# A hash-attention and gated feed-forward kernel: x of the last but one pair in a ring place, and other steps where the two stages meet

## The chip, the cores and the metric

The kernel runs on one core of a Trainium2 chip. The metric is the device time of one execution in microseconds (us); the lower, the better.

## The reference

Two blocks follow each other, all in fp32:

```python
q_bits = (einsum('bhsd,dk->bhsk', q, proj) > 0)       # 6 bits; the same for k
mask = q_bucket[:, :, :, None] == k_bucket[:, :, None, :]
scores = where(mask, q @ k.T / sqrt(64), -1e9)
attn = softmax(scores)                                # + 1e-9 in the denominator
x = (attn @ v).transpose(0, 2, 1, 3).reshape(3072, 512)
out = (silu(x @ w_gate) * (x @ w_val)) @ w_out
```

q, k and v are 4 batches x 8 heads x 768 x 64; w_gate and w_val are 512 x 1536, w_out is 1536 x 512.

## The kernel before, in words

The order of instructions on every engine is the order in which the program writes them (a manual schedule); semaphores do the rest.

**Attention.** The work goes by pairs of heads: 4 batches x 4 pairs, n = 0 to 15. For each pair, TensorE (PE) forms scores in 12 units (2 halves of 384 queries x 6 chunks of 128 keys, `score`, line 550), ACT takes the exponential (line 560), DVE adds the weights up (`add`, lines 599 to 606), and PE multiplies them with v (`attend`, line 581). Pair 0 is special: q and k land in two halves each, are copied into `qraw` and `kraw` (`start_first`, line 470), are transposed on PE (line 485), and are copied to `qT` and `kT` (lines 489 and 492).

The softmax denominators take a way of their own. `total(n)` sums them on PE (line 617), `fetch_row` copies the row on ACT (622) and sends it by DMA to `few`; `invert` takes the reciprocal on DVE (630), sends it to DRAM (`sums`) and loads it back spread over the partitions, by two DMAs, into the tile `r` (639). `norm` then scales x of that pair on DVE (646), and for pairs of batch 1 to 3 stores it in DRAM (`xram`, line 650). The list `waiting` holds inversions still to come, `last` scalings still to come; `settle` turns the first into the second, `finish` runs a list.

**Preparing the weights.** The weights come as doubles, in 36 pieces of 128 x 512. Each is loaded into a `words` tile, scaled on ACT (lines 139, 140), widened on DVE (lines 153, 155, 158: "widening", `widen_pieces`), rounded on ACT (146), split on DVE into parts (166, 168), and stored in DRAM as `ram`. In the attention this is done in batches (`begin_pieces`, `widen_pieces`, `keep_pieces`); in the gated block `turns()` gives it out in single steps, seven for each piece. In all, 22 pieces are kept when the gated block begins.

**Gated block.** Tokens go in blocks of 1024 (3 blocks). An order written out by hand alternates up steps U (12 per block, each with a gate half and a value half of 24 matmuls: 16 into `a`, 8 into `n`) and down products D (after U3, U6, U9 and U11; 8 chunks of 9 matmuls each into one tile `o` of two PSUM banks; the last one of a block starts four chunks ahead). All products come from one pool `pp` of four such tiles. After the first half of an up step, ACT copies `a` (779), DVE subtracts `n` (785); after the second, DVE multiplies the two (789), ACT writes `hid` (790), and two more DVE steps on `hid` (796, 799) are put off until after the next atom. Each chunk of a first down product is copied by ACT (840) and finished by DVE (846).

Each of these pieces of work, two per half of an up step and one per chunk, is an "atom" and counts one in `count[0]`. After each atom a number of preparing steps is given out, from the tuple by `kind`. The list `left` holds what remained of the attention's inversions and scalings; it is taken up at atoms 6 and 14.

**Ring.** Weights for PE are loaded from `ram` by POOL's queue into a ring of six places (`bring`, line 251), three in a pool of the whole kernel and three in `late_ring`, a pool in memory that the attention held. `hid`, `gate` and `val` lie in the attention's memory too. Three pieces are brought in the last three rounds of the attention, three at the start of the gated block, and one after each half of an up step, three after each down product. POOL's queue also carries the weight loads and stores of the attention; SP's queue carries q, k, v, the small DMAs of the denominators, and later the weights (`queues[0]`).

Of the kernel before, what the change touches and what calls it, by code (L numbers as in the profile page):

```python
# [8 lines left out]
FP32 = mybir.dt.float32  # L9
# [10 lines left out]
def kernel(  # L20
# [20 lines left out]
    nc = tc.nc  # L41
# [62 lines left out]
    n = 0  # L104
# [136 lines left out]
    def bring(count=1):  # L241
        for _ in range(count):
            i = len(held)
            if i == len(wanted):
                return
            what, n = wanted[i]
            at = place[what, n % NF]
            assert progress["kept"] > at, (i, at, progress)
            pool = ringp[i % sum(RINGS) >= RINGS[0]]
            held[what, n] = t = pool.tile([P, 3, PIECE], FP32R, tag="ring", name="ring")  # L250
            nc.gpsimd.dma_start(t.bitcast(FP32), ram[at].bitcast(FP32))  # L251

# [52 lines left out]
    def attention(scope):  # L305
# [127 lines left out]
        def front(n):  # L433
            bits["q", n] = sides["q", n % 2]
            bits["k", n] = sides["k", n % 2]
            low, high = slice(0, BLOCK), slice(D, D + BLOCK)

            def hash_blocks(todo):
                tile_ = joint(n - 2)[:, 1]
                for i, (name, half) in enumerate(todo):  # L440
                    nc.tensor.matmul(tile_[i * BLOCK : (i + 1) * BLOCK, 0:HQ], hash_w,  # L441
                                     T[name, n][:, half * HQ : (half + 1) * HQ],
                                     start=True, stop=True)

                def sign(i, name, half, to=low, **how):
                    nc.scalar.activation(bits[name, n][to, half * HQ : (half + 1) * HQ],
                                         tile_[i * BLOCK : (i + 1) * BLOCK, 0:HQ], AF.Sign,
                                         **(how or {"bias": nudge[name]}))

                return [lambda i=i, at=at, **how: sign(i, *at, **how) for i, at in enumerate(todo)]  # L450

            def spread_k(times, cols=slice(0, S)):
                b = bits["k", n][:, cols]
                for to, by in ((high, times[1]), (low, times[0])):
                    nc.vector.tensor_scalar(b[to], b[low], scalar1=by, scalar2=None, op0=ALU.mult)

            def spread_q():
                nc.scalar.dma_start(bits["q", n][high], bits["q", n][low])

            def hash_next(todo):  # L460
                q0, q1, k0, k1 = hash_blocks(todo)
                return [q0, q1, spread_q, k0, k1, lambda: spread_k(times_k)]

            def transpose_blocks(name):
                T[name, n] = opnd.tile([P, S], FP32, tag=name + "T", name=name + "T")
                nc.vector.transpose(T[name, n], raws[name, n].rearrange("p c h d -> p (c h d)"))

            def start_first():
                def copy(how, name, at):
                    how(raws[name, n].rearrange("p c h d -> p h c d")[:, :, at],  # L470
                        landing[name][:, :, at])

                copy(nc.scalar.copy, "k", slice(0, 1))
                copy(nc.vector.tensor_copy, "k", slice(1, CH))
                copy(nc.vector.tensor_copy, "q", slice(0, CH))
                copy(nc.vector.tensor_copy, "k", slice(CH, NCH))
                copy(nc.vector.tensor_copy, "q", slice(CH, NCH))
                for half in range(2):
                    cols = slice(half * HQ, (half + 1) * HQ)
                    for name in "kq":  # L480
                        if not half:
                            T[name, n] = opnd.tile([P, S], FP32, tag=name + "T", name=name + "T")
                        ps = two_banks("tps")[:, 0]
                        for i in range(CH):
                            nc.tensor.transpose(ps[:, i * P : (i + 1) * P],
                                                raws[name, n][:, half * CH + i].rearrange("p h d -> p (h d)"),
                                                ident)
                        if name == "k":
                            nc.scalar.activation(T[name, n][:, cols], ps[:, 0:HQ], AF.Copy,
                                                 scale=2 / OFF)  # L490
                        else:
                            nc.vector.tensor_copy(T[name, n][:, cols], ps[:, 0:HQ])

                tile_ = joint(n - 2)[:, 1, 0:HQ]
                products(0)
                hash_blocks([("k", 0), ("q", 0), ("k", 1), ("q", 1)])
                signs = twos[-1][:, 1, 1, 0 : HQ // 2].bitcast(BF16)
                nc.scalar.activation(signs, tile_, AF.Sign, bias=every[:, 0:1])

                def spread(half, at):  # L500
                    rows = slice(2 * half * BLOCK, (2 * half + 1) * BLOCK)
                    to = slice(half * HQ + at.start, half * HQ + at.stop)
                    for i, here in enumerate((low, high)):
                        nc.vector.tensor_scalar(bits["k", n][here, to], signs[rows, at],
                                                scalar1=every[rows, 1 + i : 2 + i], scalar2=None,
                                                op0=ALU.mult)

                def copy_q(half, copy, here):
                    rows = slice((2 * half + 1) * BLOCK, (2 * half + 2) * BLOCK)
                    copy(bits["q", n][here, half * HQ : (half + 1) * HQ], signs[rows])  # L510

                copy_q(0, nc.scalar.copy, low)
                spread(0, slice(0, P))
                copy_q(0, nc.vector.tensor_copy, high)
                spread(0, slice(P, HQ))
                spread(1, slice(0, HQ))
                for here in (low, high):
                    copy_q(1, nc.vector.tensor_copy, here)
                products(1)
                products(2)  # L520
                mark(0)
                products(3)
                for i in range(1, 4):
                    mark(i)

            order = [("q", 0), ("q", 1), ("k", 0), ("k", 1)]
            if n:
                return [lambda name=name: transpose_blocks(name) for name in "kq"] + [
                    lambda: hash_next(order)]
            return start_first()  # L530
# [3 lines left out]
        av = {}  # L534
        xT = {}
        mean = {}
        waiting = []

        def weights(u):
# [33 lines left out]
        def attend(u):  # L573
# [7 lines left out]
                nc.tensor.matmul(ps[h * D : (h + 1) * D, 0:width], raws["v", n][:, h, c, :],  # L581
                                 a[:, h, 0:width], start=c == 0, stop=c == NCH - 1)
            if (half, c) == (1, NCH - 1):
                pool, tag = (xp, "xT") if n < len(pairs) - 1 else (lastp, "last")
                xT[n] = pool.tile([P, S], FP32, tag=tag, name=tag)
                mean[n] = small.tile([P, 1], FP32, tag="e", name="e")
                nc.scalar.activation(mean[n], av[n][:, 0, HQ : HQ + 1], AF.Copy, scale=EPS)
                nc.scalar.copy(xT[n].rearrange("p (x q) -> p x q", x=2), av[n][:, :, 0:HQ])
# [40 lines left out]
        def invert(n, few):  # L629
# [2 lines left out]
            nc.sync.dma_start(s, few)  # L632
            if n == len(pairs) - 1:
                t = homes[-1].tile([P, 2, DM], FP32, tag=f"o{NP - 1}", name="o")[:, :, 0:HQ]
            else:
                t = att.tile([P, 2, HQ], FP32, tag="r", name="r", bufs=1)
            flat = s.rearrange("p e -> (p e)").rearrange("(h x t) -> h (x t)", h=2, t=HQ)
# [37 lines left out]
        for n in range(len(pairs)):  # L675
# [4 lines left out]
            if n and more:  # L680
                steps = front(n + 1)
                prepare_pair(2)
            widen_pieces()
            settle()
            for i in range(2 * NCH):
                if u + i > 3:
                    score(u + i)
# [21 lines left out]
                attend(u + c)  # L709
            load(n + 2, "v")  # L710
            keep_pieces()
            if n >= len(pairs) - 3:
                bring()
        widen_pieces()
        settle()
        total(len(pairs) - 1)()
        finish(last)
        left.extend(waiting)

    left = []  # L720
    homes = []
# [6 lines left out]
    def gated_block(scope):  # L728
# [39 lines left out]
        def atoms_of(kind, n):  # L768
            if kind == "U":
# [5 lines left out]
                for what, z in (("g", gate), ("v", val)):  # L775
# [5 lines left out]
                    def other(what=what, z=z):  # L781
                        _, second, _, n_ = ops[what]
                        second()
                        bring()
                        nc.vector.tensor_tensor(two(z), two(z), n_, op=ALU.subtract)  # L785
                        if what == "g":
                            nc.scalar.activation(z, z, AF.Silu)  # L787
# [104 lines left out]
                    yield chunk  # L892

        bring(RINGS[1])
        queues[0] = nc.sync
        tails = []
        splits = []
# [20 lines left out]
        for kind, n in order:  # L918
# [12 lines left out]
            for at, atom in enumerate(atoms_of(kind, n)):  # L931
# [12 lines left out]
                        for x in more:  # L944
                            x.pop(0)()
                count[0] += 1
                if left and count[0] in (6, 14):
                    left.append(left.pop(0)())
                    left[:] = [f for f in left if f]
                for _ in range(((1, 2, 2, 2) if kind == "U" else (1, 2, 2) + (1,) * 9)[at]):  # L950
                    step = next(mine, None)
                    if step:
                        step()
# [35 lines left out]
```

## Time and profile before

| | us |
|---|---|
| time before, median of 3 (909.69 to 911.08) | 910.63 |
| the profiled execution: its own time | 911.15 |
| the profiled execution: its span | 909.3 |
| PE busy in the span | 902.5 |
| DVE busy | 665.9 |
| ACT busy | 449.7 |
| POOL busy | 90.3 |
| gated block's first matmul | 314.22 |
| PE's last matmul ends | 903.70 |

The span goes from the first to the last instruction; the time has 1.85 us more around it. PE's busy time is made of modelled ends, so the distance between starts says more than the busy share. In lines of the timeline the first number is the start, the second the duration, both in us; the bracket gives the idle time of that engine just before and what ended it.

### The profile page before, as it was taken

To read this page: it belongs to the slowest core of one execution; us is meant where nothing else is said; L and a number is where in the kernel's file an instruction comes from. 1 tells how busy PE (TensorE), PEld (TensorE's weight loads), DVE (VectorE), ACT (ScalarE), POOL (GpSimd) and SP (SyncE) were. 2 spreads that over 40 slices of the span, in tenths; PEclk is the share of its full clock that TensorE was granted. 3 is DMA by queue.
4 is the path that set the end of the run, shared out by engine and by line. 5 is a ranking of instruction groups with operands and counts; after the bars stand their busy time and mean duration, and the time that the engine had idled before them with its cause. 6 is when DMAs were issued, how large, how long until landed. Compare 5 with 4: busy or idle time off the path is not lost.

```text
span 909.3 us, 12462 instructions
## 1 busy us (share of the span) xinstructions
PE 902.5 (99%) x4801; PEld 638.0 (70%) x4801; DVE 665.9 (73%) x785; ACT 449.7 (49%) x603; POOL 90.3 (10%) x186
## 2 busy tenths in 40 slices
PE   9999999999999999999999999999999999999998
PEld 5444444444444588788888888888888888888886
DVE  6779999999988868778786856365658754474746
ACT  6688989788887645452514233331313243413220
POOL 2001100011001210000100000101000100001000
PEclk9999999999999999999999999999999999999999
DMA  7566777878876699776756563444434642515332
GB/s 183 106 152 184 188 204 185 211 213 227 225 192 202 214 386 334 263 273 239 275 184 240 207 249 105 174 139 164 148 139 160 238 147 98 202 70 208 104 139 93
DMA packets 143706, 174.24 MB, mean 192 GB/s; under 512 B 103360, under 2 KB 113568, under 8 KB 143648
## 3 DMA queue, kind: packets, MB, share of 16 engines
q0 software_dynamic: 22240, 114.83, 35.6%
q1 hardware_dynamic: 120000, 57.43, 24.2%
q10 hardware_dynamic: 1408, 1.20, 0.5%
q8 instruction: 38, 0.62, 0.3%
q14 instruction: 20, 0.16, 0.1%
HBM read 133.17 MB, written 39.42 MB: 190 GB/s over the span
## 4 chain that ended last, share of the span: by engine, by line
PE 90%; DVE 4%; DMA 3%; ACT 1%; issue 1%; SPq 0%; ACTq 0%; DVEq 0%
PE a L740 26%; PE o L740 20%; PE sc L550 16%; PE n L740 13%; PE av L581 12%; DMA r<-sums 1%; PE joint L617 1%; PE joint L441 1%; DMA sums<-few 1%; DMA xram<-xT 1%; DVE hid L796 1%; DVE stage L155 0%; PE idle L375 0%; DVE v L789 0%; DVE v L785 0%
## 5 line engine op out<-in xcount | busy, mean ns | idle before, releaser
L740 PE MATMUL a<-xparts,ring 128*128 128x512 f32 x1152 | 273.1, 389 | 0.4 <-DMA ring<-ram 0.4
L740 PEld LDWEIGHTS a<-xparts,ring 128*128 128x128 f32 x1152 | 216.1, 188 | 46.1 <-issue 1.4
L740 PE MATMUL o<-ring,hid 128*128 128x512 f32 (+1 forms) x870 | 199.0, 389 | 1.4 <-DVE o L846 1.2
L740 PEld LDWEIGHTS o<-ring,hid 128*128 128x128 f32 x870 | 162.7, 188 | 36.1 <-DVE o L846 2.7
L560 ACT ACTIVATE A<-sc 128x768 f32<-128x768 f32 x192 | 154.0, 814 | 1.5 <-PE sc L550 0.7
L550 PE MATMUL sc<-qT,kT 64*128 64x384 f32 x768 | 153.0, 483 | 0.1
L740 PE MATMUL n<-xparts,ring 128*128 128x512 f32 x576 | 142.2, 389 | 0.0
L581 PE MATMUL av<-A,vraw 128*64 128x386 f32 (+1 forms) x768 | 127.7, 489 | 0.0
L740 PEld LDWEIGHTS n<-xparts,ring 128*128 128x128 f32 x576 | 108.1, 188 | 22.4
L785 DVE TENSOR_TENSOR v<-v,n 128x1024 f32<-128x1024 f32 x36 | 44.0, 1221 | 99.8 <-PE n L740 97.9
L251 POOL DMA_DIRECT2D ring<-ram x108 | 56.9, 529 | 498.4 <-PE n L740 311.9
L581 PEld LDWEIGHTS av<-A,vraw 128*64 128x64 f32 x768 | 53.7, 137 | 73.3 <-issue 63.0
L779 ACT ACTIVATE g<-a 128x1024 f32<-128x1024 f32 x36 | 36.9, 1025 | 127.2 <-PE a L740 126.5
L550 PEld LDWEIGHTS sc<-qT,kT 64*128 64x128 f32 x768 | 68.9, 187 | 40.1 <-issue 35.2
L790 ACT ACTIVATE hid<-v 128x1024 fp32r<-128x1024 f32 x36 | 38.2, 1062 | 109.0 <-DVE v L789 106.4
L787 ACT ACTIVATE g<-g 128x1024 f32<-128x1024 f32 x36 | 38.2, 1062 | 90.1 <-DVE g L785 90.1
L846 DVE TENSOR_TENSOR o<-o 128x512 f32<-128x512 f32 x92 | 63.1, 687 | 19.2 <-ACT o L840 16.9
L785 DVE TENSOR_TENSOR g<-g,n 128x1024 f32<-128x1024 f32 x36 | 43.8, 1216 | 34.4 <-PE n L740 34.4
L550 PE MATMUL sc<-qb,kb 64*128 64x384 bf16 x384 | 63.5, 323 | 0.0
L796 DVE SCALAR_TENSOR_TENSOR hid<-hid,v 128x1024 fp32r<-128x1024 f32 (+1 forms) x39 | 44.5, 1141 | 19.7 <-ACT hid L790 19.7
L599 DVE SCALAR_TENSOR_TENSOR both<-A 128x1536 f32<-128x1536 f32 x32 | 55.4, 1732 | 4.2 <-ACT A L560 2.8
L603 DVE TENSOR_TENSOR both<-both,A 128x1536 f32<-128x1536 f32 x32 | 55.9, 1748 | 1.7
(86 smaller groups left out, 694.4 us busy)
## 6 DMA issues: line engine op xcount, KB each, us to landing
ring<-ram POOLq DMA_DIRECT2D x108, 768.0 KB, 4.8
ram<-stage POOLq DMA_DIRECT2D x22, 768.0 KB, 4.4
ram<-stage SPq DMA_DIRECT2D x14, 768.0 KB
vraw<-in_v_dram SPq DMA_DIRECT2D x16, 384.0 KB
out_dram<-o SPq DMA_DIRECT2D x23, 256.0 KB
kraw<-in_k_dram SPq DMA_DIRECT2D x60, 96.0 KB
qraw<-in_q_dram SPq DMA_DIRECT2D x60, 96.0 KB
r<-sums SPq DMA_DIRECT2D x30, 192.0 KB
```

The costliest lines, as they stand in the source:

```text
L251: nc.gpsimd.dma_start(t.bitcast(FP32), ram[at].bitcast(FP32))
L550: nc.tensor.matmul(banks_of[u][:, h], x["k", n][rows, ks], x["q", n][rows, qs], start=start, stop=stop)
L560: nc.scalar.activation(weights(u)[:, :, 0:HQ], banks_of.pop(u), AF.Exp, scale=SCALE * (1.0 if units[u][0] else OFF / 2))
L581: nc.tensor.matmul(ps[h * D : (h + 1) * D, 0:width], raws["v", n][:, h, c, :], a[:, h, 0:width], start=c == 0, stop=c == NCH - 1)
L599: nc.vector.scalar_tensor_tensor(out=t, in0=first, scalar=S * EPS / P / 2, in1=now, op0=ALU.add, op1=ALU.add)
L603: nc.vector.tensor_tensor(t, t, now, op=ALU.add)
L740: nc.tensor.matmul(ps, w, x, start=start, stop=stop)
L785: nc.vector.tensor_tensor(two(z), two(z), n_, op=ALU.subtract)
L787: nc.scalar.activation(z, z, AF.Silu)
L790: nc.scalar.activation(h, val, AF.Copy, scale=TOWARD / STEP)
L796: nc.vector.scalar_tensor_tensor(out=l_, in0=h_.bitcast(FP32), scalar=-STEP, in1=v_, op0=ALU.mult, op1=ALU.add)
L846: nc.vector.tensor_tensor(accs[c], accs[c], t[:, 1], op=ALU.subtract)
```

## The change

Six things are changed, and the rest stays as it was.

1. In pair 0, ACT makes both copies of k, DVE both of q, and q is transposed first.
2. x of pair 14 (the last but one) and its reciprocals lie in one tile of the ring's first pool, instead of in the attention's `xp` and `r`. The scaling of that pair (`norm`) goes into `left` and is taken up in the gated block.
3. In the last round of the attention `settle` stands ahead of `widen_pieces`. At the end, the widening stands behind the first ring loads of the gated block.
4. Two ring loads instead of three are issued in the attention. The pools are met in another order, the load after U0's value half is dropped, and two loads are issued after atom 4.
5. `left` is taken up at atoms 4, 6 and 11 instead of 6 and 14: the scaling of pair 14, the inversion of pair 15, the scaling of pair 15.
6. Down products give out fewer preparing steps: the first (0, 0, 0, 2, 1, 2, 2, 2), all others (0, 0, 1, 0) and then one per atom, instead of (1, 2, 2) and then one per atom. The steps that are not given out there follow later.

```diff
-            pool = ringp[i % sum(RINGS) >= RINGS[0]]
+            pool = ringp[2 <= i % sum(RINGS) < 2 + RINGS[1]]
...
-                copy(nc.scalar.copy, "k", slice(0, 1))
-                copy(nc.vector.tensor_copy, "k", slice(1, CH))
-                copy(nc.vector.tensor_copy, "q", slice(0, CH))
-                copy(nc.vector.tensor_copy, "k", slice(CH, NCH))
-                copy(nc.vector.tensor_copy, "q", slice(CH, NCH))
+                for here in (slice(0, CH), slice(CH, NCH)):
+                    copy(nc.vector.tensor_copy, "q", here)
+                    copy(nc.scalar.copy, "k", here)
                 for half in range(2):
                     cols = slice(half * HQ, (half + 1) * HQ)
-                    for name in "kq":
+                    for name in "qk":
...
             if (half, c) == (1, NCH - 1):
-                pool, tag = (xp, "xT") if n < len(pairs) - 1 else (lastp, "last")
-                xT[n] = pool.tile([P, S], FP32, tag=tag, name=tag)
+                if n == len(pairs) - 2:
+                    t = ringp[0].tile([P, 3, PIECE], FP32R, tag="ring", name="late")
+                    t = t.bitcast(FP32).rearrange("p a b -> p (a b)")
+                    xT[n], lent[n] = t[:, 0:S], t[:, S : 2 * S]
+                else:
+                    pool, tag = (xp, "xT") if n < len(pairs) - 1 else (lastp, "last")
+                    xT[n] = pool.tile([P, S], FP32, tag=tag, name=tag)
...
+            elif n in lent:
+                t = lent[n].rearrange("p (x q) -> p x q", x=2)
             else:
                 t = att.tile([P, 2, HQ], FP32, tag="r", name="r", bufs=1)
...
-            widen_pieces()
-            settle()
+            if more:
+                widen_pieces()
+                settle()
+            else:
+                settle()
+                widen_pieces()
...
-            if n >= len(pairs) - 3:
+            if len(pairs) - 3 <= n < len(pairs) - 1:
                 bring()
-        widen_pieces()
         settle()
         total(len(pairs) - 1)()
-        finish(last)
-        left.extend(waiting)
+        left.extend(last + waiting)
...
-                        bring()
+                        if (what, n) != ("v", 0):
+                            bring()
...
         bring(RINGS[1])
+        widen_pieces()
...
-                if left and count[0] in (6, 14):
+                if left and count[0] in (4, 6, 11):
                     left.append(left.pop(0)())
                     left[:] = [f for f in left if f]
-                for _ in range(((1, 2, 2, 2) if kind == "U" else (1, 2, 2) + (1,) * 9)[at]):
+                    if count[0] == 4:
+                        bring(2)
+                if kind == "U":
+                    pace = (1, 2, 2, 2)
+                elif n == 0:
+                    pace = (0, 0, 0, 2, 1, 2, 2, 2)
+                else:
+                    pace = (0, 0, 1, 0) + (1,) * 8
+                for _ in range(pace[at]):
```

More of the change, by code (lines that the diff above doesn't have):

```diff
@@ L536, in attention @@
         mean = {}
+        lent = {}
         waiting = []
```

## The prediction

> **What bounds the kernel now.** I read the busy table first (PE 902.5 us of a span of 909.3), then the chain of waits, then the timelines of PE, DVE, ACT and POOL where the chain leaves PE. The chain runs through PE except around 290 to 373 us. PE's waits by sum are only 1.2 us (for DVE, line 846) and 0.4 us (for a ring load), but a matmul's end in these records is modelled, so I take starts instead:
>
> ```profile
> 314.22 3.92 PE L740 MATMUL a<-xparts,ring 128*128 128x512 f32 x16
> ...
> 319.79 3.79 PE L740 MATMUL a<-xparts,ring 128*128 128x512 f32 x16
> ...
> 325.76 3.91 PE L740 MATMUL a<-xparts,ring 128*128 128x512 f32 x16 [0.37 <-DMA ring<-ram]
> ...
> 331.32 3.79 PE L740 MATMUL a<-xparts,ring 128*128 128x512 f32 x16
> ...
> 358.52 10.73 PE L740 MATMUL o<-ring,hid 128*128 128x512 f32 x45
> 370.49 6.85 PE L740 MATMUL o<-ring,hid 128*128 128x512 f32 x27 [1.24 <-DVE o L846]
> 377.18 3.79 PE L740 MATMUL a<-xparts,ring 128*128 128x512 f32 x16
> ```
>
> An undisturbed down product takes 16.32 us in the chain (72 matmuls, 0.2267 each), so the 24 matmuls of one half of an up step should take 5.44. Start to start the first four halves take 5.57, 5.97, 5.56 and 5.44. The second and third lose 0.53 + 0.12 = 0.65 us around the late ring load; 0.13 is lost in the first, at the change of stage. The first down product (D0) runs from 358.52 to 377.18 = 18.66: it loses 2.34 us, not 1.24. From there to 903.70 the chain is PE without a gap, at the same pace. So PE's work is fixed, and what can be won in this region is 0.65 + 2.34 = 2.99 us. Where both come from:
>
> ```profile
> 324.95 1.02 DVE L646 SCALAR_TENSOR_TENSOR xT<-xT,e,r 128x768 f32<-128x768 f32 x1 [6.28 <-DMA r<-sums]
> 325.89 1.21 DVE L785 TENSOR_TENSOR g<-g,n 128x1024 f32<-128x1024 f32 x1
> ...
> 369.15 0.69 DVE L155 SCALAR_TENSOR_TENSOR stage<-words,stage 128x512 int32<-128x512 int32 x1
> 369.75 0.68 DVE L846 TENSOR_TENSOR o<-o 128x512 f32<-128x512 f32 x1
> 370.35 0.69 DVE L158 CUSTOM_DVE_ANT_0 stage<-words,stage 128x1024 uint16<-128x1024 uint16 x1
> ```
> ```profile
> 332.82 1.06 ACT L790 ACTIVATE hid<-v 128x1024 fp32r<-128x1024 f32 x1 [2.60 <-DMA xram<-xT]
> ...
> 365.55 1.06 ACT L840 ACTIVATE o<-o 128x512 f32<-128x512 f32 x2
> 371.07 0.63 ACT L146 ACTIVATE stage<-stage 128x512 fp32r<-128x512 f32 x1 [4.46 <-DVE stage L158]
> 371.61 0.58 ACT L840 ACTIVATE o<-o 128x512 f32<-128x512 f32 x1
> ```
>
> DVE stands 6.28 us before the scaling of pair 14 (line 646); the first subtraction of the gated block, whose matmuls ended by 319.8, starts only at 325.89. ACT then waits 2.60 us until x of pair 14 has been stored, since `hid` lies in its memory. DVE never makes that good before D0: its U3 subtraction of `v` starts at 362.06, 3.5 us after PE. D0 has four PSUM tiles. Chunk 5 waits for chunk 1, whose end on DVE stands behind the two `hid` steps and a preparing step (369.15); chunk 6 waits for chunk 2, whose ACT copy stands behind a preparing step (line 146) that waits for line 158 (371.61).
>
> **What the Trainium skill says.** "Perfetto Trace Analysis", Tensor Engine Instruction: the profiler's end of a matmul is an estimate. The trace agrees: it shows 389 ns for a matmul that comes every 227, and hides 1.10 of D0's 2.34 us. "PSUM — Partial Sum Buffer", Engine vs sequencer instructions: ACT, DVE and GpSimd queues are strict FIFO. The trace agrees: the ready copy of chunk 2 stood behind line 146 until 371.61. "DMA: Bandwidth & Descriptors", Queues, rings and completion order: each DMA engine takes turns between queue rows at packet granularity, so SP's small transfers share with POOL's bulk. The trace agrees: `sums<-few` took 2.12 us on idle engines at 312.54, 7.13 us at 299.92.
>
> **The change, part by part.**
> *Startup.* q goes first, and ACT makes both copies of k. Before, the last operand of the first scores was qT on DVE (6.28, 0.56 us; scores at 6.98). Now q's transposes come first, kT follows on ACT at about 6.3 with 0.49 (its row before). ACT's copy of the second half of k starts when it lands, 5.46, and takes about 0.5 (nearest row: ACT's 128x384 copy at line 622, 0.48), so it ends at about 5.95, before kT. Gain 0.07; I take 0, with bounds of -0.3 and +0.3 since landings vary.
> *Inversion ahead of the widening (iteration 15).* The reciprocal of pair 13 passes six preparing steps: from 299.67 to 295.9, 3.8 us. The scaling of pair 13 at 311.13 waited 1.91 us for it; now it follows the sum at 309.2. All behind it on DVE, including the ends of two prepared pieces that POOL stores at 314.12 and 315.45, comes 1.9 us sooner.
> *Ring loads.* Piece 2 (U1's gate) was issued by POOL at 316.00 and waited for until 325.7. It now follows the second store at once: 315.45 - 1.9 + 0.6 = 314.1, with pieces 3 and 4 behind it and two weight loads after them instead of before. Everything queued ahead of it on POOL also moves by 1.9, so I expect landing at about 323.8, against a need at about 325.2. Gain 0.65; ends 0 (DMA share was 1.0 from 316 on; a slower queue can eat 1.4 us) and 0.65.
> *Pair 14 in a ring place.* The same 1.02 us on DVE, and the same two loads on SP and one store. It moves behind the product of `v` in U0, to about 327.7; its reciprocals landed at 324.85 before and now are asked for 1.9 us sooner, so cover is at least 2.8 us. DVE's first subtraction goes to 319.8, and the 2.60 us of ACT vanish, as `hid` no longer lies over that x. If the loads came later than 327.7, U0's `hid` would be late next.
> *Pair 15 from atom 14 to atom 11*, that is, from U3 to U2 on DVE, 1.01 us. Its sum chain follows the reciprocal after U1's first subtraction, which moves from 338.06 to about 333.5. Before, `sums` took from 338.31 to 344.12, and the packets of its reciprocals are seen until 349.4; so now about 345. DVE reaches the scaling at about 344.8. Cost: a wait of 0.2 us, bounds 0 and 4. Queued behind it: `v` of U2, needed by PE (its PSUM tile, U3's second half) only at about 356; so up to 4 us cost PE nothing directly, but come back as lag at D0.
> *D0's pace (0, 0, 0, 2, 1, 2, 2, 2).* By the changed order DVE ends chunks 1, 2 and 3 straight after `hid`, and ACT copies five chunks before line 146. With the old lag chunk 1 would end at 369.15 + 0.7 = 369.85 against 368.72 (PE's need): loss about 1.2 and the gain 1.1. Laying DVE's and ACT's rows end to end in the changed order, from 319.8 on, puts U3's subtraction at 358.7 (3.4 sooner: no 6.28 us stall, pair 15 out of U3); then chunk 1 ends at about 366.7, and PE loses nothing. Gain 2.34, ends 1.1 and 2.34.
> *D1 to D3: 5 and 9 steps instead of 10 and 14.* No step is dropped; each takes DVE or ACT about 0.4 to 0.7 us. Up steps keep 7. D1 and D2 had no PE loss before, so nothing to gain; the last piece is kept at the start of U10 instead of in D2. Cover: the ring load of the last piece is needed in the fourth down product, over 20 us later. Cost 0; if that cover went, PE would wait there for a load of about 15 us.
> *New wait.* Ring load 7 (U3's `v`, in the lent place) waits on POOL for pair 14's store; the loads of D0 queue behind it. Store at about 328.7 plus the 6.84 us of the old one: 335.5, instead of 331.78. In this window ring loads took 6.5 to 18.6 us, so it lands at 342 to 354, needed at 352.3. Cost 0, ends 0 and 2.
>
> Sum: 0.65 + 2.34 = 2.99, less 0.2 for a remainder at either place: 2.8 us. The profiled execution took 911.15 (909.3 and 1.85 around it): 908.35. It stands 0.52 above the median of 910.63, so the median becomes 907.8.
>
> **The rivals.**
> *Half of it:* pair 15's scaling in U2 waits until 350 or later (its loads under a full DMA), DVE's lag stays, and only the new order in D0 helps: 0.65 + 1.1 = 1.75, 908.9. For it: DMA is full from 316 to 366. Against: DVE's cover of 4 us.
> *Nothing moves:* piece 2 still late and the lag kept by both waits, 910 to 911. Against: the 6.28 us were shown to have one cause.
> *Slower:* ring load 7 becomes PE's wait at U3. It stands behind a store that stands behind DVE, and D0's three pieces stand behind it. It decides once the load lands after 352.3; to be slower than before by over 1.8 us it must eat 2.8 as well, landing at 356.9 or later, 21 us after its issue, with about 912.5 and up. Against: the longest load in the window was 18.6.
> *The change doesn't do what it says:* pair 14's scaling is in the second half of U0, not in U1. If its loads still were late there, the stall would only move by 2 us; then 910.
>
> **How the numbers follow.** Full gain 0.68 (907.2 to 908.7), half 0.15, nothing 0.06, slower 0.11 (ring load 7, or startup and preparation together). A measurement of this kernel can tell about 0.2%, 1.82 us, from no change. Full gain passes it except with a later startup; half falls just inside. Faster 0.70, same 0.19, slower 0.11. Range 906.9 to 910.2: the first two cases with the startup's bounds and part of the third.
>
> **What would show it.** Right: PE's halves of U0 and U1 at 5.44, D0 at about 16.3; no wait before DVE's first subtraction; ACT's `hid` in U0 by 328; line 146 in D0 behind five copies. Wrong: a PE wait for a ring load in U1 or U3, a long DVE wait at pair 15's scaling, or any PE gap after D0.

## The result, and the profile after

| | before | after |
|---|---|---|
| median of 9 runs each, us | 910.15 (909.45 to 911.08) | 907.83 (907.58 to 908.52) |
| the profiled execution, its own time / span | 911.15 / 909.3 | 907.61 / 905.8 |
| first scores of pair 0 | 6.98 | 6.47 |
| gated block's first matmul | 314.22 | 313.70 |
| PE's loss in U0 to U3, after the first half | 0.65 | 0 |
| PE's loss in D0 | 2.34 | 0 |

The ratio is 0.9974, 95% interval [0.9964, 0.9984]: 1.5 to 3.3 us of 910.15. The two profiled executions lie further apart, 3.54 us. Of these, 0.65 + 2.34 = 2.99 are the two losses, 0.51 is an earlier start of the first scores, 0.04 is spread over the rest.

The chain that ended last leaves PE hardly at all now (the line gives shares of the span by engine; before it named DVE with 4% and DMA with 3%):

```profile
PE 99%; DVE 0%; DVEq 0%; issue 0%
```

PE's timeline where it lost time before:

```profile
313.70 3.94 PE L748 MATMUL a<-xparts,ring 128*128 128x512 f32 x16
...
319.30 3.79 PE L748 MATMUL a<-xparts,ring 128*128 128x512 f32 x16
...
324.74 3.79 PE L748 MATMUL a<-xparts,ring 128*128 128x512 f32 x16
...
330.18 3.79 PE L748 MATMUL a<-xparts,ring 128*128 128x512 f32 x16
...
357.38 16.48 PE L748 MATMUL o<-ring,hid 128*128 128x512 f32 x72
373.70 3.79 PE L748 MATMUL a<-xparts,ring 128*128 128x512 f32 x16
```

Start to start: 5.60, 5.44, 5.44 for the halves of U0 and U1 (0.16 stays at the change of stage), and 16.32 for D0. The 72 matmuls of D0 stand in one row, without a break.

DVE in the same stretch (the bracket is its idle time and what ended it):

```profile
308.62 1.01 DVE L652 SCALAR_TENSOR_TENSOR xT<-xT,e,r 128x768 f32<-128x768 f32 x1
...
319.56 1.22 DVE L794 TENSOR_TENSOR g<-g,n 128x1024 f32<-128x1024 f32 x1 [3.40 <-PE n L748]
...
327.41 1.01 DVE L652 SCALAR_TENSOR_TENSOR late<-late,e 128x768 f32<-128x768 f32 x1
...
333.40 0.22 DVE L634 RECIPROCAL few<-few 128x12 f32<-128x12 f32 x1
...
346.93 1.02 DVE L652 SCALAR_TENSOR_TENSOR last<-last,e,o 128x768 f32<-128x768 f32 x1 [2.46 <-DMA o<-sums]
...
358.85 1.22 DVE L794 TENSOR_TENSOR v<-v,n 128x1024 f32<-128x1024 f32 x1 [0.22 <-ACT v L787]
...
365.94 1.88 DVE L855 TENSOR_TENSOR o<-o 128x512 f32<-128x512 f32 x3
```

The scaling of pair 13 (308.62) no longer waits, the first subtraction (319.56) waits for PE and not for a DMA, and the scaling of pair 14 (`late`, 327.41) finds its reciprocals there. The only wait for a DMA is new: 2.46 us ahead of pair 15's scaling. U3's subtraction of `v` starts 1.47 us behind the first matmul of D0 (358.85 against 357.38), and the chunks 1 to 3 of D0 follow straight after `hid`. Before, it was 3.54 us behind (362.06 against 358.52):

```profile
362.06 1.22 DVE L785 TENSOR_TENSOR v<-v,n 128x1024 f32<-128x1024 f32 x1 [0.22 <-ACT v L779]
```

ACT, and POOL's ring loads:

```profile
328.15 1.06 ACT L799 ACTIVATE hid<-v 128x1024 fp32r<-128x1024 f32 x1 [3.99 <-DMA few<-row]
...
362.33 1.06 ACT L849 ACTIVATE o<-o 128x512 f32<-128x512 f32 x2
363.70 0.60 ACT L849 ACTIVATE o<-o 128x512 f32<-128x512 f32 x1 [0.30 <-PE o L748]
365.74 0.60 ACT L849 ACTIVATE o<-o 128x512 f32<-128x512 f32 x1 [1.44 <-PE o L748]
367.78 0.60 ACT L849 ACTIVATE o<-o 128x512 f32<-128x512 f32 x1 [1.44 <-PE o L748]
369.18 0.63 ACT L146 ACTIVATE stage<-stage 128x512 fp32r<-128x512 f32 x1 [0.80 <-DVE stage L158]
```
```profile
313.79 1.58 POOL L251 DMA_DIRECT2D ring<-ram  x3 [0.29 <-issue]
...
335.97 1.57 POOL L251 DMA_DIRECT2D ring<-ram  x3 [10.24 <-DVE stage L166]
```

U0's `hid` starts at 328.15 instead of 332.82. What ends ACT's wait there is, by the profile, the DMA of pair 15's row into `few`; in a second profile of the same kernel it is the product on DVE, and `hid` starts at 327.44. In D0 five copies (x2, then three) stand ahead of the preparing step of line 146, and from the third on ACT waits for PE, no longer the reverse. U1's gate is loaded from 313.79 instead of 316.00; the load into the lent place is issued at 335.97. Before, these were DVE's scaling of pair 13, with its wait, and POOL's load of U1's gate:

```profile
311.13 1.02 DVE L646 SCALAR_TENSOR_TENSOR xT<-xT,e,r 128x768 f32<-128x768 f32 x1 [1.91 <-DMA r<-sums]
```
```profile
316.00 0.53 POOL L251 DMA_DIRECT2D ring<-ram  x1
```

### The profile page after: what moved, and what is told of

Same layout as the page of the kernel before. It is cut to its first block, busy times and chain, and to the rows that moved or that the text cites. A ratio compares the mean times of both kernels' runs of the same rounds, so it can differ in the third digit from the quotient of the medians.

```text
span 905.8 us, 12457 instructions
## 1 busy us (share of the span) xinstructions
PE 900.9 (99%) x4801; PEld 637.6 (70%) x4801; DVE 665.2 (73%) x783; ACT 450.5 (50%) x604; POOL 90.1 (10%) x186
## 4 chain that ended last, share of the span: by engine, by line
PE 99%; DVE 0%; DVEq 0%; issue 0%
PE a L748 29%; PE o L748 21%; PE sc L549 17%; PE n L748 14%; PE av L580 14%; PE joint L621 1%; PE joint L441 1%; PE idle L375 0%; PE tps L483 0%; DVE o L843 0%; DVE o L851 0%; DVE o L883 0%; DVEq L1002 0%; DVE kb L369 0%
```

## The experiments

Two theories were to be told apart. **Mine**: DVE's stall for the reciprocals of pair 14 becomes a lag of DVE behind PE, which D0 pays for through its four PSUM tiles; the deferral removes the stall, the new pace moves the point where D0 begins to pay, and an earlier issue of one ring load saves the rest. **The rival**: a part of this alone (order in D0, startup, the place, the order ahead of the widening) carries the gain, or a new wait eats it. "Lag" below is the start of U3's `v` subtraction on DVE, less the start of D0 on PE.

**Before and after once more.** No edit.

> The kernel before, unchanged, against itself. It says how much of the 3.54 us between the two profiled executions (911.15 and 907.61) belongs to the one execution that was shown, as the medians are only 2.3 apart. If the losses of the first profile (2.34 us in D0, 0.65 around the late ring load, scores starting at 6.98) are fixed by the order of work, the new profile has them again within 0.1 us each and a time near 910.6 to 911.1. If they depend on when transfers land, one of them is smaller by 0.5 us or more and the time is nearer 909.5 to 910.2. Time 910.2, ratio 1.000.

Before: 910.98 us, ratio 1.0002 [0.9994, 1.0011]. Its profile (own time 912.45) shows another loss at the same ring load, PE's timeline:

```profile
320.12 3.79 PE L740 MATMUL a<-xparts,ring 128*128 128x512 f32 x16
323.75 1.97 PE L740 MATMUL n<-xparts,ring 128*128 128x512 f32 x8
327.24 3.91 PE L740 MATMUL a<-xparts,ring 128*128 128x512 f32 x16 [1.52 <-DMA ring<-ram]
```

That half takes 7.12 instead of 5.44, a loss of 1.68. The load was issued at 317.35 and there by 327.2, after 9.9 us; in the first profile it took 9.7 from 316.00. The 0.65 us that I had read was one draw. What varied was less the length of the load than its issue: pair 13's scaling on DVE had waited 2.95 us for its reciprocals here, against 1.91 in the first profile (more on this below).

> The changed kernel, unchanged, once more. If the losses where the stages meet are gone by the order of work and not by luck, the new profile again has 5.44 us for every half of U0 to U3 after the first and 16.3 for D0, and all that differs is when the first scores start (6.4 to 7.0). Then the spread of its times comes from the startup alone: 907.5 to 908.6, median 907.9.

After: 907.76 us, 0.9969 [0.9959, 0.9980]. Lag 1.56, no loss in U0 to U3 or in D0.

**Startup alone** (part 1, on the kernel before).

```diff
+                for here in (slice(0, CH), slice(CH, NCH)):
+                    copy(nc.vector.tensor_copy, "q", here)
+                    copy(nc.scalar.copy, "k", here)
...
-                    for name in "kq":
+                    for name in "qk":
```

> Only the startup is changed: ACT makes both copies of k, DVE both of q, q goes first. The prediction had 0.07 us for this and took 0. The profile after shows the first scores at 6.47 instead of 6.98. If that is the change's doing, the scores start at 6.45 to 6.55 here and the time falls by 0.5 us, to about 909.7, with D0 and the ring load as lossy as before. If it is scatter of landings, the start lies anywhere from 6.5 to 7.0 and the time doesn't move by more than 0.2.

910.88 us, 1.000 [0.9992, 1.0008]; the first scores start at 6.70. It shows no gain, but a gain of some tenths would not be seen in times. Over all profiles the start splits in two groups, by how long the first three transposes took (some 0.86 or 0.52 us, in kernels of either order). With the slow ones the mean is 7.14 (old order, 3 profiles) and 6.97 (new, 5), with the fast ones 6.63 (old, 3) and 6.39 (new, 3). So by the profiles the order seems to bring about 0.2 us, and chance moves the start by about 0.5; the starts of the two orders overlap where the transposes were slow.

**D0's pace alone, and the other down products' pace alone** (part 6 in halves, on the kernel before).

```diff
+                elif n == 0:
+                    pace = (0, 0, 0, 2, 1, 2, 2, 2)
+                else:
+                    pace = (1, 2, 2) + (1,) * 9
```

> Only D0's preparing steps are changed to (0, 0, 0, 2, 1, 2, 2, 2); the lag of DVE stays, and so do the late ring load and the scaling of pair 14 ahead of the first subtraction. Theory of the prediction: the order alone gives 1.1 of D0's 2.34 us, since chunk 1 still ends at about 369.85 against 368.72; D0 takes 17.5 us instead of 18.66, time about 909.1. Rival: the order is all of it, D0 takes 16.3 to 16.5, time about 908.0. Second rival: the lag is all of it, D0 stays above 18.3 and the time is that of before.

909.99 us, 0.9996 [0.9988, 1.0004]. PE's timeline of D0:

```profile
358.06 8.32 PE L740 MATMUL o<-ring,hid 128*128 128x512 f32 x36
366.61 2.35 PE L740 MATMUL o<-ring,hid 128*128 128x512 f32 x9 [0.23 <-DVE o L846]
369.61 6.46 PE L740 MATMUL o<-ring,hid 128*128 128x512 f32 x27 [0.65 <-DVE o L846]
375.90 3.79 PE L740 MATMUL a<-xparts,ring 128*128 128x512 f32 x16
```

D0 takes 17.84, a loss of 1.52 where it was 2.34, at a lag of 3.72. The new pace helps the old lag, but doesn't pay for it. After the first four chunks, all of PE's waits are still for DVE's `o`.

> The kernel before with only the paces of the down products after D0 changed: 5 and 9 preparing steps instead of 10 and 14. The prediction costs it at 0: no PE loss before in D1 to D3, and the last piece is stored 20 us before its ring load is needed. So PE has no gap after D0, and the time is that of before within 0.3 us (scatter of its ring load and startup). Rival: steps that end up in U10 collide with the splitting of the next block's x, and PE loses time at U10 or U11.

With (0, 0, 1, 0) and then ones for the others only: 910.76 us, 0.9995 [0.9987, 1.0003]. D0 loses 2.35 as before. After D0, PE has no gap over 0.1 us. From the end of D0 to the last down product it took 511.51 us (376.70 to 888.21), against 511.36 before (377.18 to 888.54): the steps put off cost at most 0.15 us in these two profiles and win nothing.

**The change without its startup and its paces** (parts 2 to 5), **and without the startup only** (parts 2 to 6).

> Everything but the startup and the paces: pair 14 in the ring place, the inversion ahead of the widening, the new order of ring loads, atoms 4, 6 and 11. Theory of the prediction: the ring load is in time (0.65 us), and DVE is about 3 us less behind at D0. In the profile after, U3's subtraction of v is at 358.85 instead of 362.06; with the old pace chunk 1 would then end at about 367.3 against a need at 367.6, and chunk 2's copy behind line 146 at 369.1 against 369.6: D0 loses 0 to 0.4 us even so, and the time is about 907.6 to 908.0 plus the startup, 908.0 to 908.4. Rival: without the new pace D0 still loses 1 us or more; time about 909.

908.72 us, 0.9981 [0.9974, 0.9989]. PE's timeline:

```profile
357.45 17.09 PE L750 MATMUL o<-ring,hid 128*128 128x512 f32 x72
374.38 3.79 PE L750 MATMUL a<-xparts,ring 128*128 128x512 f32 x16
```

16.93 us start to start: D0 loses 0.61 with the old pace, at a lag of 1.77, a little more than I had expected. Nothing is lost in U0 to U3 after the first half. Most of the gain is here.

> The changed kernel with the startup of before (k's first chunk on ACT, all else on DVE, k transposed first). If the startup's change is worth nothing, as the run of it alone said (ratio 1.000), the time is that of the changed kernel within 0.2 us, 907.9. If it is worth the 0.5 us seen between two profiles, 908.4. D0 takes 16.3 us: the new pace takes away the 0.61 us that were left with the old one.

908.49 us, 0.9975 [0.9965, 0.9985]; lag 2.29, and D0 loses 0.05. By the traces the new pace takes away the last half microsecond, though the lag is larger here; the medians of the two are too near to show it. This kernel and the kernel after differ in the startup alone, and the median of the latter, measured in the same set of runs, is 0.7 us lower (907.76, ratio 0.9969). The intervals of the two ratios overlap, but it is what I had expected of a startup worth half a microsecond, and more than the 0.2 us of the profiles.

**The place without the deferral.** Pair 14 lies in the ring place, but is scaled at the end of the attention, ahead of the widening.

```diff
-        left.extend(last + waiting)
+        finish(last)
+        left.extend(waiting)
...
-                if left and count[0] in (4, 6, 11):
+                if left and count[0] in (6, 11):
...
-                    if count[0] == 4:
-                        bring(2)
+                if count[0] == 4:
+                    bring(2)
```

> The changed kernel, pair 14 in its ring place, but its scaling ahead of the gated block's first subtraction, as before the change. DVE stands at it until its reciprocals land (about 321 to 323), and the widening comes behind it, so the first subtraction starts at 325 to 327 instead of 319.56. ACT does not wait for that x to be stored, as it lies outside the memory of hid. Theory: the lag of DVE, not the place, is what D0 pays for. Then U3's subtraction of v is at 361 or later, D0 loses 1 to 2 us in spite of the new pace (1.52 with the new pace alone), and the time is 909.0 to 909.8. Rival: the place is what matters (ACT's wait for the store), then D0 loses nothing and the time stays at 907.9.

911.16 us, 1.0003 [0.9995, 1.0011]: all of the gain is gone, more than I had expected. DVE's timeline, and then PE's around D0:

```profile
321.06 1.02 DVE L652 SCALAR_TENSOR_TENSOR late<-late,e 128x768 f32<-128x768 f32 x1 [8.24 <-DMA late<-sums]
...
325.78 1.21 DVE L795 TENSOR_TENSOR g<-g,n 128x1024 f32<-128x1024 f32 x1
...
363.44 1.22 DVE L795 TENSOR_TENSOR v<-v,n 128x1024 f32<-128x1024 f32 x1 [0.22 <-ACT v L788]
```
```profile
358.30 2.20 PE L749 MATMUL o<-ring,hid 128*128 128x512 f32 x9
...
377.53 3.79 PE L749 MATMUL a<-xparts,ring 128*128 128x512 f32 x16
```

The stall is back (8.24 us), the first subtraction is back at 325.78 (325.89 before), the lag is 363.44 - 358.30 = 5.14, and D0 loses 2.91 in spite of the new pace. Another 0.47 us is lost in U1. The stall is what brings the loss back, and the deferral is what removes it. Not all of the 5.14 us need come from it: pair 15's scaling in U2 waits 1.71 us for its reciprocals here too.

**The scaling later** (atom 8, in U1's end, with pair 15 at 9 and 14, and the ring loads that wait for the place at atom 8). This pushes the loads into the lent place back, which is the mechanism of my slower rival.

```diff
-                        if (what, n) != ("v", 0):
+                        if (what, n) not in (("v", 0), ("v", 1)):
...
-                if left and count[0] in (4, 6, 11):
+                if left and count[0] in (8, 9, 14):
...
-                    if count[0] == 4:
-                        bring(2)
+                    if count[0] == 8:
+                        bring(3)
```

> The changed kernel with all that is left of the attention taken up later: pair 14's scaling at atom 8 (end of U1) instead of 4, pair 15's inversion at 9 and its scaling at 14; ring loads 7, 8 and 9 follow at atom 8. It is the slower rival of the prediction, made to happen: the lent place comes free about 11 us later. Scaling at about 338.5, its store issued at 339.7, ring load 7 at about 346 to 347 (335.97 in the profile after). PE needs it at 351.9. Theory: a ring load in this window takes 6 to 12 us, so PE waits 0.5 to 6 us at the second half of U3, and the time is 908.5 to 914. Rival: by then the queue is empty and the load takes under 5 us; PE waits for nothing, time 907.9.

910.44 us, 0.9998 [0.9990, 1.0006]. POOL, and then DVE:

```profile
342.14 2.10 POOL L251 DMA_DIRECT2D ring<-ram  x4 [16.51 <-DVE hid L805]
```
```profile
359.54 1.02 DVE L652 SCALAR_TENSOR_TENSOR last<-last,e,o 128x768 f32<-128x768 f32 x1 [4.81 <-DMA o<-sums]
...
362.76 1.22 DVE L794 TENSOR_TENSOR v<-v,n 128x1024 f32<-128x1024 f32 x1 [0.22 <-ACT v L787]
```

The ring loads went out at 342.14, six microseconds later than in the kernel after, and PE still began U3's `v` half at 351.83 without a wait. So the slower rival didn't come. The gain was lost elsewhere: pair 15's scaling, now in U3, waits 4.81 us for its reciprocals, and U3's subtraction (362.76) stands behind it in DVE's queue. So does a preparing step that started only at 360.47, and behind that one, on ACT, the copy of `v` that the subtraction needs. The trace so agrees again with the strict order within an engine's queue that "PSUM — Partial Sum Buffer" of the Trainium skill states under Engine vs sequencer instructions. The lag is 5.49, D0 loses 3.30.

**The widening first again** (part 3 undone in the last round), **pair 15 at atom 14 again**, **and both.** The first edit, and the second:

```diff
-            if more:
-                widen_pieces()
-                settle()
-            else:
-                settle()
-                widen_pieces()
+            widen_pieces()
+            settle()
...
-                if left and count[0] in (4, 6, 11):
+                if left and count[0] in (4, 6, 14):
```

> The changed kernel with the widening ahead of the inversion again in the last round of the attention. Pair 13's reciprocal, its scaling and the two stores that POOL has in front of ring load 2 come 1.5 to 1.9 us later. Theory: these stores set when ring load 2 lands, so U1's first half waits 0 to 1 us for it again (ring load issued at about 315.3 instead of 313.8), time 907.9 to 908.6. Rival: the two weight loads that now stand behind the ring loads were what held it up, then PE waits for nothing and the time is that of the changed kernel.

910.91 us, 1.0001 [0.9994, 1.0007]: again nothing is left of the gain, which neither theory had. DVE's timeline:

```profile
335.66 0.22 DVE L634 RECIPROCAL few<-few 128x12 f32<-128x12 f32 x1
...
351.70 1.02 DVE L652 SCALAR_TENSOR_TENSOR last<-last,e,o 128x768 f32<-128x768 f32 x1 [4.97 <-DMA o<-sums]
...
363.61 1.22 DVE L790 TENSOR_TENSOR v<-v,n 128x1024 f32<-128x1024 f32 x1 [0.21 <-ACT v L783]
```

Lag 363.61 - 358.49 = 5.12, D0's loss 2.88, and 0.52 in U0 to U3. There the profile names no releaser, but the ring load of U1's gate was issued late again, at 316.51.

> The changed kernel with pair 15's scaling at atom 14 again instead of 11. In the profile after, DVE stood 2.46 us at that scaling in U2 (344.47 to 346.93), where the prediction had 0.2. Theory: that wait is lag of DVE which D0 could still bear (chunk 1 ended 1.0 us ahead of the need), so taking it away moves U3's subtraction 1 to 2 us forward, but not PE: 5.44 for every half, 16.3 for D0, time 907.8 within 0.2. Rival: the scaling in U3 puts 1 us back right ahead of D0 and PE loses up to 0.7 there; time 908.2 to 908.6.

907.97 us, 0.9968 [0.9957, 0.9980], with no wait at pair 15's scaling (355.28), a lag of 0.37 and no loss. So the 2.46 us of the kernel after cost PE nothing. This was the version that might have beaten the kernel after; it is its equal.

> The kernel after with the old order in the last round of the attention (widening ahead of the inversion), as in a_widen_first, and with pair 15's scaling taken up at atom 14 instead of 11. a_widen_first lost all of the gain: 0.52 us at the ring load in U1 and 2.88 us in D0, with DVE 5.12 us behind PE at U3 and 4.97 us of waiting for o at pair 15's scaling in U2. Theory: that wait carries the loss into D0. Taken up at atom 14 the loads are there, the wait is under 1 us, DVE's lag at U3 falls to 0.3 to 1.5 us, D0 loses at most 0.6 us, and what stays is about 0.5 us at the ring load: 908.0 to 909.0. Rival: the late start of the gated block itself (pair 13's scaling at 311.3, ACT's hid in U0 at 330.4 instead of 328.2) carries on to U3; then the lag stays over 3 us, D0 loses over 2 us, and the time is 910.5 or more.

908.18 us, 0.9973 [0.9966, 0.9980]. DVE's timeline:

```profile
355.42 1.01 DVE L652 SCALAR_TENSOR_TENSOR last<-last,e,o 128x768 f32<-128x768 f32 x1
...
358.64 1.22 DVE L790 TENSOR_TENSOR v<-v,n 128x1024 f32<-128x1024 f32 x1 [0.23 <-ACT v L783]
```

Lag 0.83, no loss in D0, though ACT's `hid` in U0 starts at 329.41. So the wait at atom 11 did most of the harm in the kernel with the widening first, and not the late start. Its lag is 3.65 us above that of the kernel after (5.12 against 1.47): 2.51 of them are the longer wait (4.97 against 2.46), and 1.14 that U1's first subtraction comes later, reckoned from the start of D0. One reservation: in this profile the reciprocals of pair 13 came 1.3 us sooner than in that one, by chance, and the ring load was issued at 315.02, so that the 0.52 us are missing too. The medians, 2.7 us apart in 21 and 18 runs (2.5 by the ratios to the kernel before, measured beside each), don't rest on that draw.

**All profiles in one table.** Lag and loss in D0, in us, by the pace of D0:

| kernel | pace | lag | D0's loss | lag less loss |
|---|---|---|---|---|
| before | old | 3.54 | 2.34 | 1.20 |
| before, again | old | 3.16 | 1.99 | 1.17 |
| startup alone | old | 3.12 | 1.93 | 1.19 |
| others' pace alone | old | 3.54 | 2.35 | 1.19 |
| without startup and paces | old | 1.77 | 0.61 | 1.16 |
| D0's pace alone | new | 3.72 | 1.52 | 2.20 |
| without startup | new | 2.29 | 0.05 | 2.24 |
| widening first | new | 5.12 | 2.88 | 2.24 |
| place without deferral | new | 5.14 | 2.91 | 2.23 |
| scaling later | new | 5.49 | 3.30 | 2.19 |
| after, after again | new | 1.47, 1.56 | 0 | - |
| widening first, atom 14 | new | 0.83 | 0 | - |
| atom 14 | new | 0.37 | 0 | - |

D0's loss is the lag less about 1.18 with the old pace, and the lag less about 2.22 with the new one; below that it is nothing (seen with the new pace only). The two constants are read from these same profiles; all ten that lost time keep to them within 0.03 us. The new pace is worth 1.04 us where the lag is large, and the rest must come from the lag.

## Why the prediction was right, point by point

**The bound, and what could be won.** 2.99 us were counted from starts, 2.99 came back in the two profiles. The median fell by 2.3 where the prediction had 2.8; by the ratio of the second set of runs it fell by 2.8 (0.9969 of 910.97). The forecast of 907.8 met 907.83 more closely than its steps deserve: it was reckoned from a median of 910.63, and that of the nine runs is 910.15.

**Startup**, taken as 0 within 0.3: about 0.2 by the groups of profiles, 0.7 by the medians of the kernel after with and without it, and nothing by the kernel before with it alone. The 0.51 us between the two profiles is mostly the chance length of the transposes. What the startup is worth stays open, and it may lie outside the bounds.

**Inversion ahead of the widening.** Predicted: reciprocal of pair 13 at 295.9, scaling following the sum at 309.2. The profile: 295.38 and 308.62. The step was right, its weight wasn't seen. The loads of these reciprocals went out at 297.08 instead of 307.11: the store ahead of them began 4.3 us sooner, and took 1.4 us instead of 7. I priced the step by the ring load and by cover at pair 14. It matters at pair 15 too. With the widening first, the reciprocal of pair 15 starts at 335.66 instead of 333.40, but DVE comes to the scaling at atom 11 just as much later, so this alone would not lengthen the wait. In all six profiles with the inversion at atom 6 and the scaling at 11, DVE comes to the scaling 11.1 us after the start of the reciprocal, and the wait is what the transfers take beyond that: the reciprocals were there after 13.5 us in the kernel after, after 16.0 with the widening first. Why they were slower there is not shown.

**Ring loads.** Issue at 314.1 predicted, 313.79 seen; gain 0.65, and no profile with the inversion first shows PE waiting for that load. The term was mis-sized as one draw: in four more profiles with the old issue order the halves U0 to U3 lost 1.80, 1.24, 0.44 and 0. The cause of the scatter can be read from the traces. The load's issue follows the start of pair 13's scaling by 4.87 us in all five profiles with the old order, and by 5.16 or 5.17 in all nine with the new one; that scaling waited 1.56 to 2.95 us for its reciprocals in the five. So the issue came 8.2 to 9.6 us ahead of the need (the time at which PE would have begun U1's gate without a wait), and in the four of them where PE waited the load took 9.5 to 9.9. With the inversion first the scaling doesn't wait, and the load goes out 10.9 to 11.0 us ahead. This is the likely reason why the times of the kernel before are spread over 2.5 us (909.14 to 911.66 in 22 runs beside the last experiment), and those of the kernel after over 1 us (907.46 to 908.52 in 15 of its 16 runs, with one at 909.90).

**Pair 14 in a ring place.** First subtraction at 319.8 predicted, 319.56 seen; ACT's `hid` by 328, 328.15; no stall at the deferred scaling, none seen. The place without the deferral gave no gain. Whether the place was needed for the deferral was not tried: x would then lie in memory that the gated block takes.

**Pair 15 at atom 11.** The wait was mis-sized: 0.2 predicted within 0 to 4, 2.46 measured. SP sent for the reciprocals at 337.96, and they were there at 346.9, where I had expected 345: I had let the transfers take 11.5 us from the reciprocal on (333.5 to 345), and they took 13.5. That up to 4 us cost PE nothing directly and come back as lag was the right form of the price. The lag with which they come back was 1.5, under the 2.22 of the new pace.

**D0's pace.** Predicted: 1.1 of gain and about 1.2 of loss left with the old lag, nothing lost with the new lag. Measured: 1.04, and 3.54 - 2.22 = 1.32. U3's subtraction at 358.7 predicted, 358.85 seen; that is luck in part. The scaling of pair 15 came 1.9 us later than reckoned (346.93 against 344.8 + 0.2), and from it to U3's subtraction the prediction had 13.7 us where the profile has 11.92.

**D1 to D3** at 0, and the **new wait** at 0: both seen, D1 to D3 within 0.15 us. Load 7 at 335.5 predicted, 335.97 seen.

**The rivals.** The slower one was given too much: its load could go out at 342.14 and still be in time. "Half of it" was given the wrong price. Its case, pair 15's scaling held until 350 or later, is what the kernel with the widening first does (351.70), and it ran at 910.91, not at 908.9: I had let the old lag stay, where such a wait made a larger one, 5.12, which takes back what the new pace gives. "Nothing moves" has the place without the deferral and that same kernel for its examples, each with a long wait of DVE for reciprocals (8.24 and 4.97 us). That the stall would only move by 2 us didn't come: pair 14's scaling (327.41) found its reciprocals there.

**A reading that was wrong.** The prediction has the 2.12 us of the store at 312.54 on idle DMA engines. Their busy share in that stretch was 0.52, against 0.79 at 299.92. The two lengths fit engines that are shared, but don't show that they take turns by the packet.

## What to carry to other kernels

Read what a busy engine loses from the distances between starts, and look for how far its partner is behind where the buffers are fewest: here one number, DVE's lag at D0, gave the loss to within 0.03 us in ten profiles, with one constant, read from them, for each order of work. A small transfer's consumer that stands in a queue ahead of critical work should be put as far behind the transfer's start as its own deadline allows (with pair 15's inversion at atom 6, its scaling at atom 14 didn't wait with either order ahead of it, and at atom 11 waited 1.7 to 5.0 us; at atom 14, but with the inversion at 9, it waited 4.8). A load that is just in time in one profile is a scatter in the times; one profile of before doesn't give its price.

## What the runs showed that I had not expected

Small transfers varied far more than their size suggests. The reciprocals of one pair, 6 KB, were stored in 1.4 us at 295.62 in the kernel after, and in some 7 us at 299.92 in the one before; the DMA engines' busy share was 0.31 and 0.79 in these stretches. The two loads of pair 15, 192 KB each, took 9.0 us from their issue in the kernel after and 10.7 with the widening first, with the DMA engines full in both. The store of pair 13's reciprocals in the kernel with the widening first took 7.1 us from 300.02, and 6.0 us from 299.84 where only a later atom differed: its length changes from run to run.

The first three transposes took 0.85 to 0.88 us in eight of the profiles and 0.52 to 0.58 in the others, in kernels of either order, with the granted clock shown as full in both. The 15 matmuls named `idle`, which PE makes ahead of them, took 4.02 us in those eight profiles and 3.59 to 3.84 in the other six, so by the profile PE was slower there already. What decides it stays open; it moves the first scores by about half a microsecond.
